# Spectral filter and gated FFN on one core: the stores of two FFT stages issued by ACT instead of SP

## The chip, the cores and the metric

The kernel runs on one core of one Trainium2 chip. The metric is the device time of the whole program in microseconds (us); lower is better. The kernel before takes 1571.36 us, the median of 3 runs (1568.31 to 1573.47).

## What is computed

Eight sequences of 3136 positions and 256 channels (`x`, float32) pass through two blocks. The first multiplies each channel's spectrum by a learned filter:

```python
X = np.fft.rfft(x, axis=1)
y = np.fft.irfft(X * (filt_r + 1j * filt_i)[None], n=3136, axis=1)
```

The second is a gated feed-forward block with a three-tap convolution along the sequence, width 1024 in the middle:

```python
h = np.maximum(y @ w_in, 0.0)
conv_out = sum(conv_w[k] * hp[:, k:k + S] for k in range(3))   # hp: h padded by one on each side
out = (h * sigmoid(conv_out)) @ w_out
```

## The kernel before

**The spectral part.** Each FFT of 3136 points is taken as 28 x 112 and done by matrix products with constant tables, in three stages that follow one another per sequence ("batch", b = 0 to 7). A batch is cut into 14 pieces of two columns (p = 0 to 13); one piece is a tile of 112 partitions x 512 float32, 224 KB. Between the stages the data must change its layout from one kind of row to another, and that is done by a trip through DRAM:

- **First stage** (`first`, matmul L321): a piece `x` is loaded from the input (L304), multiplied into a PSUM tile `ps`, copied by ACT into an SBUF tile `sa` (L309) and stored to the DRAM tensor `a_dram` of its batch (L315).
- **Second stage** (`second`, L328, for the last piece of a batch L331): a piece `a` is loaded from `a_dram` (L304) across all the rows of the batch. So the first `a` load of a batch can start only when all 14 `sa` stores of that batch have landed. Its product `pp` is multiplied by the filter on DVE (L340 to L342) and added on POOL to `z` (L344).
- **Third stage** (`third`, L351): `z` is multiplied into another `ps`, copied by ACT to `sb` (L309) and stored to `b_dram` (L315).
- **Last stage** (L216): pieces `br` are loaded back from `b_dram`, multiplied, and split by ACT (L146) and DVE (L149) into two halves `y` for the next block. For batch 0 this runs at the end of the spectral part, for the others inside the FFN part.

**The loop.** One loop of 135 steps (`i`, L369) runs all of it as a pipeline. In step i the first stage works on piece i - 1 counted over all batches, the second on piece i - 19, the third on piece i - 22. A step in the middle holds one matmul group of each stage, two ACT copies, one group of DVE and POOL work, and four transfers: load `x`, load `a`, store `sb`, store `sa`. In its first third the loop also loads the tables and the filter, and about every twelve steps a pair of weight pieces `raw` (256 KB each, L263).

**Buffers.** `x` has 8 tiles, `a` 5, `sa` and `sb` 4 each, and the PSUM tiles `ps` 5, shared by the first and third stages. An `x` load of step i waits until PE has done the first stage of the same step, because that frees its tile. An `a` load of step i is used by the second stage of step i + 4.

**What sets the order.** PE, ACT, DVE and POOL run their instructions in the order of the code (`manual_schedule` with `COMPUTE`, L368 and L527). SP runs only transfers, and their order is made by the tile framework, which simulates the program and lets SP take what it thinks is ready first. An engine's queue is strictly in order: a transfer whose wait is not met holds back everything behind it on that engine. Each transfer reports its landing on one of eight counters (DMAHW0 to DMAHW7), taken in turn over all transfers of the program in the framework's order, whichever engine issues them; a transfer waits until the one before it on its counter has landed. So about eight transfers can be under way.

**The FFN part** (from L494 on) runs from about 386 us to the end and is not touched by the edit.

Of the kernel before, what the change touches and what calls it, by code (L numbers as in the profile page):

```python
# [124 lines left out]
def tile_fft_filter_gated_ffn(  # L125
# [16 lines left out]
    nc = tc.nc  # L142
# [85 lines left out]
    with (  # L228
# [66 lines left out]
        def pool(kind):  # L295
            return xp if kind in ("x", "sa") else fp
# [10 lines left out]
        def store(kind, b, p, ps):  # L307
            st = pool(kind).tile([112, 2, D], F32, name=kind, bufs=4)
            nc.scalar.activation(st, ps, AF.Copy)  # L309
            sl = slice(2 * p, 2 * p + 2)  # L310
            if kind == "sa":
                v = a_dram[b][sl].rearrange("n p d -> p n d")
            else:
                v = b_dram[b].rearrange("n (r g) d -> (n r) g d", g=G)[:, sl]
            nc.sync.dma_start(out=v, in_=st)  # L315

        def first(b, p):
            r = rows.pop(("x", b, p))
# [49 lines left out]
        with tc.manual_schedule(engines=COMPUTE):  # L368
            for i in range(NI):  # L369
# [25 lines left out]
                if pt is not None:  # L395
                    store("sb", *at(m - 4), pt)
                if pf is not None:
                    store("sa", *at(f - 1), pf)
# [167 lines left out]
```

## Time and profile before

| | |
|---|---|
| Median of 3 runs | 1571.36 us |
| The profiled execution | 1572.45 us |
| its span in the trace | 1570.7 us |
| PE busy | 1505.0 us, 96% |
| DVE busy | 1280.6 us, 82% |
| ACT busy | 1189.3 us, 76% |
| Spectral part | 0 to about 386 us |
| of it with all three stages at work | about 80 to 326 us |

Busy times are sums over the span. A matmul's end is modelled, so PE's busy time is not PE at its peak; the distance from one matmul group's start to the next is the safer number. A row of SP's queue (SPq) shows the time in which SP issues a transfer, not the time in which the data moves.

### The profile page before, as it was taken

Reading aid. Unit: us, or ns where it says so; the run is one execution under the profiler, and the core shown is the slowest. Engines: PE = TensorE matmul, PEld = TensorE weight load, DVE = VectorE, ACT = ScalarE, POOL = GpSimd, SP = SyncE. Lnnn points to the kernel's source line nnn. Section 1 sums busy time; section 2 is a strip of 40 time slices with the busy share of each in tenths; the row PEclk is TensorE's granted clock in tenths of the full one; section 3 lists DMA queues with packets and bytes.
Section 4 is the critical chain, followed back from the end, with each engine's and each line's share of the span. In section 5 each row is a group of like instructions: output and inputs, shape, how many; then the busy total and the mean of one; then the engine's idle time right before and its main releaser. Section 6 shows DMA issues by size and latency. Waiting matters only on the chain.

```text
span 1570.7 us, 26429 instructions
## 1 busy us (share of the span) xinstructions
PE 1505.0 (96%) x9424; PEld 1346.7 (86%) x9424; DVE 1280.6 (82%) x1965; ACT 1189.3 (76%) x2162; POOL 697.4 (44%) x624
## 2 busy tenths in 40 slices
PE   5699999988999999999999999999999999999998
PEld 3356666656999999999999999999999999999998
DVE  0478888888888888888888888888888888888887
ACT  3444444435888888888888888888888888888887
POOL 0255555553444444444444444444444434444444
PEclk9799999999999999999999999999999999999999
DMA  9999999984111011111101111111111111100001
GB/s 285 288 321 337 342 342 346 328 283 140 30 48 48 30 48 48 48 48 48 47 25 36 48 53 48 47 45 47 36 42 48 48 43 36 48 25 24 24 25 48
DMA packets 128278, 166.83 MB, mean 106 GB/s; under 512 B 10682, under 2 KB 87571, under 8 KB 128147
## 3 DMA queue, kind: packets, MB, share of 16 engines
q1 hardware_dynamic: 128147, 165.14, 33.0%
q8 instruction: 75, 1.23, 0.3%
q14 instruction: 56, 0.46, 0.1%
HBM read 88.03 MB, written 77.07 MB: 105 GB/s over the span
## 4 chain that ended last, share of the span: by engine, by line
PE 83%; DMA 10%; DVE 3%; issue 1%; ACT 1%; SPq 1%; POOL 1%; ACTq 0%; DVEq 0%; POOLq 0%
PE ps_h L178 12%; PE ps_h L179 12%; PE ps_h L177 11%; PE po L473 11%; PE po L475 11%; PE po L474 11%; PE ps_h L216 6%; DMA a<-a_dram 4%; PE pp L328 3%; PE ps L351 3%; PE ps L321 2%; DMA a_dram<-sa 2%; DMA t_sb<-in_fi 1%; DVE y L149 1%; DVE v L341 1%
## 5 line engine op out<-in xcount | busy, mean ns | idle before, releaser
L152 POOL TENSOR_TENSOR g<-t,g 128x448 fp32r<-128x448 f32 x448 | 517.2, 1154 | 666.9 <-ACT g L146 262.8
L473 PE MATMUL po<-wo,g 128*128 128x256 f32 x1568 | 441.6, 282 | 0.0
L475 PE MATMUL po<-wo,g 128*128 128x256 f32 x1568 | 433.9, 277 | 0.0
L474 PE MATMUL po<-wo,g 128*128 128x256 f32 x1568 | 433.6, 277 | 0.0
L447 DVE SCALAR_TENSOR_TENSOR t<-ps_h,cw,t 128x448 f32<-128x448 f32 x448 | 305.5, 682 | 83.2 <-ACT t L442 72.9
L178 PE MATMUL ps_h<-y,wi 128*128 128x450 f32 x896 | 330.4, 369 | 4.5 <-DVE y L149 4.5
L177 PE MATMUL ps_h<-y,wi 128*128 128x450 f32 x896 | 328.8, 367 | 3.0 <-ACT y L146 1.6
L179 PE MATMUL ps_h<-y,wi 128*128 128x450 f32 x896 | 328.8, 367 | 0.0
L448 DVE SCALAR_TENSOR_TENSOR t<-ps_h,cw,t 128x448 f32<-128x448 f32 x448 | 306.4, 684 | 16.0
L442 ACT ACTIVATE t<-ps_h,cw 128x448 f32<-128x448 f32 x448 | 284.8, 636 | 42.6 <-ACT ps_h L440 1.9
L473 PEld LDWEIGHTS po<-wo,g 128*128 128x128 f32 x1568 | 294.8, 188 | 7.0
L474 PEld LDWEIGHTS po<-wo,g 128*128 128x128 f32 x1568 | 294.4, 188 | 5.7
L475 PEld LDWEIGHTS po<-wo,g 128*128 128x128 f32 x1568 | 294.5, 188 | 0.0
L440 ACT ACTIVATE ps_h<-ps_h 128x450 f32<-128x450 f32 x448 | 252.0, 562 | 31.6 <-PE ps_h L179 26.8
L453 DVE TENSOR_TENSOR t<-ps_h,t 128x448 f32<-128x448 f32 x448 | 275.1, 614 | 0.1
L452 ACT ACTIVATE t<-t 128x448 f32<-128x448 f32 x448 | 255.0, 569 | 12.2 <-DVE t L448 11.2
L146 ACT ACTIVATE g<-t 128x448 fp32r<-128x448 f32 x448 | 254.6, 568 | 0.2 <-DVE t L453 0.2
L344 POOL TENSOR_TENSOR z<-u,v 120x512 f32<-120x512 f32 x112 | 157.0, 1402 | 181.4 <-DVE v L342 164.8
L309 ACT ACTIVATE sb<-ps 112x512 f32<-112x512 f32 x112 | 66.9, 597 | 161.5 <-DMA b_dram<-sb 86.7
L179 PEld LDWEIGHTS ps_h<-y,wi 128*128 128x128 f32 x896 | 168.3, 188 | 13.9
L177 PEld LDWEIGHTS ps_h<-y,wi 128*128 128x128 f32 x896 | 170.1, 190 | 11.6 <-ACT y L146 2.8
L178 PEld LDWEIGHTS ps_h<-y,wi 128*128 128x128 f32 x896 | 168.3, 188 | 13.5 <-DVE y L149 6.7
(51 smaller groups left out, 1475.0 us busy)
## 6 DMA issues: line engine op xcount, KB each, us to landing
x<-in_x SPq DMA_DIRECT2D x112, 224.0 KB, 4.9
a_dram<-sa SPq DMA_DIRECT2D x112, 224.0 KB, 4.6
a<-a_dram SPq DMA_DIRECT2D x112, 224.0 KB, 4.6
b_dram<-sb SPq DMA_DIRECT2D x112, 224.0 KB, 4.4
br<-b_dram SPq DMA_DIRECT2D x112, 224.0 KB, 2.6
out<-ot SPq DMA_DIRECT2D x27, 896.0 KB, 4.1
raw<-in_w_in SPq DMA_DIRECT2D x8, 256.0 KB, 5.2
raw<-in_w_out SPq DMA_DIRECT2D x8, 256.0 KB, 6.1
```

The lines of the kernel that those rows point to most:

```text
L152: nc.gpsimd.tensor_tensor(out=dst, in0=src, in1=hi.bitcast(F32), op=ALU.subtract)
L177: nc.tensor.matmul(ps, lhsT=wh, rhs=rh, start=start, stop=False, **kw)
L178: nc.tensor.matmul(ps, lhsT=wh, rhs=rl, start=False, stop=False, **kw)
L179: nc.tensor.matmul(ps, lhsT=wl, rhs=rh, start=False, stop=stop, **kw)
L442: nc.scalar.activation(t, h[:, 1:SUB + 1], AF.Copy, scale=cw[:, 1, f:f + 1])
L447: nc.vector.scalar_tensor_tensor(out=t, in0=h[:, 0:SUB], scalar=cw[:, 0, f:f + 1], in1=t, op0=ALU.mult, op1=ALU.add)
L448: nc.vector.scalar_tensor_tensor(out=t, in0=h[:, 2:SUB + 2], scalar=cw[:, 2, f:f + 1], in1=t, op0=ALU.mult, op1=ALU.add)
L452: nc.scalar.activation(t, t, AF.Sigmoid)
L453: nc.vector.tensor_mul(t, h[:, 1:SUB + 1], t)
L473: nc.tensor.matmul(o, lhsT=gh[:, sl], rhs=wo[0][:, f], start=first, stop=False, skip_group_check=True)
L474: nc.tensor.matmul(o, lhsT=gh[:, sl], rhs=wo[1][:, f], start=False, stop=False, skip_group_check=True)
L475: nc.tensor.matmul(o, lhsT=gl[:, sl], rhs=wo[0][:, f], start=False, stop=last, skip_group_check=True)
```

## The change

The store at the end of `store` (L315) is issued from ACT's queue instead of SP's. `store` is called for `sb` and `sa` in each step, so 224 stores move. Each one now stands on ACT directly behind the copy that fills its tile.

```diff
             if kind == "sa":
                 v = a_dram[b][sl].rearrange("n p d -> p n d")
             else:
                 v = b_dram[b].rearrange("n (r g) d -> (n r) g d", g=G)[:, sl]
-            nc.sync.dma_start(out=v, in_=st)
+            nc.scalar.dma_start(out=v, in_=st)
```

In the rows of order below, the names are those of the trace with a buffer's number: a_dram_62 is batch 5, a_dram_63 batch 6, a_dram_64 batch 7. The words in brackets are the counters that an instruction waits for: DMAHW for transfers, PE and Activation for those engines.

ACT, around the last `sa` piece of batch 5 (the 84th of 112), in the kernel before:

```order
L309 ACTIVATE sa<-ps 112x512 [waits DMAHW1_49,PE_49,Activation_49]
L309 ACTIVATE sb<-ps 112x512 [waits DMAHW4_49,PE_49,Activation_49]
L309 ACTIVATE sa<-ps 112x512 [waits DMAHW5_49,PE_49,Activation_49]
L309 ACTIVATE sb<-ps 112x512 [waits DMAHW0_49,PE_49,Activation_49]
L309 ACTIVATE sa<-ps 112x512 [waits DMAHW1_49,PE_49,Activation_49]
```

The same place on ACT in the changed kernel:

```order
L309 ACTIVATE sa<-ps 112x512 [waits PE_49]
L315 DMA a_dram_62<-sa 112x2x256 [waits DMAHW6_49,Activation_49]
L309 ACTIVATE sb<-ps 112x512 [waits PE_49]
L315 DMA b_dram_69<-sb 112x512 [waits DMAHW7_49,Activation_49]
L309 ACTIVATE sa<-ps 112x512 [waits PE_49]
L315 DMA a_dram_62<-sa 112x2x256 [waits DMAHW1_49,Activation_49]
L309 ACTIVATE sb<-ps 112x512 [waits DMAHW5_49,PE_49]
L315 DMA b_dram_69<-sb 112x512 [waits DMAHW2_49,Activation_49]
```

Each copy is followed by its store, which waits for that copy and for an earlier transfer on its counter; most copies no longer wait for a transfer themselves.

SP, at the same place, where the second stage goes from batch 4 (a_dram_61) to batch 5 (a_dram_62), in the kernel before:

```order
L304 DMA x<-in_x 112x512 [waits DMAHW6_49,PE_49]
L304 DMA a<-a_dram_61 112x512 [waits DMAHW7_49]
L315 DMA b_dram_69<-sb 112x512 [waits DMAHW0_49,Activation_49]
L315 DMA a_dram_62<-sa 112x2x256 [waits DMAHW1_49,Activation_49]
L263 DMA raw<-in_w_in 128x512 [waits DMAHW2_49,DVE_49]
L263 DMA raw<-in_w_out 128x512 [waits DMAHW3_49]
L304 DMA x<-in_x 112x512 [waits DMAHW4_49,PE_49]
L304 DMA a<-a_dram_62 112x512 [waits DMAHW5_49,DMAHW1_49]
L315 DMA b_dram_69<-sb 112x512 [waits DMAHW6_49,Activation_49]
L315 DMA a_dram_63<-sa 112x2x256 [waits DMAHW7_49,Activation_49]
L304 DMA x<-in_x 112x512 [waits DMAHW0_49,PE_49]
L304 DMA a<-a_dram_62 112x512
```

The changed kernel, from the `x` load beside the last a_dram_61 load on:

```order
L304 DMA x<-in_x 112x512 [waits DMAHW6_49,PE_49]
L304 DMA a<-a_dram_61 112x512 [waits DMAHW3_49,DMAHW0_49,PE_49]
L304 DMA x<-in_x 112x512 [waits DMAHW2_49,PE_49]
L304 DMA x<-in_x 112x512 [waits DMAHW5_49,PE_49]
L304 DMA x<-in_x 112x512 [waits DMAHW0_49,PE_49]
L304 DMA x<-in_x 112x512 [waits DMAHW7_49,DMAHW3_49,PE_49]
L304 DMA a<-a_dram_62 112x512 [waits DMAHW6_49,DMAHW7_49,DMAHW5_49,DMAHW1_49]
L304 DMA a<-a_dram_62 112x512
L304 DMA a<-a_dram_62 112x512 [waits DMAHW0_49]
L304 DMA x<-in_x 112x512 [waits DMAHW2_49,PE_49]
L304 DMA a<-a_dram_62 112x512 [waits DMAHW4_49,DMAHW3_49]
L304 DMA a<-a_dram_62 112x512 [waits DMAHW5_49,PE_49]
```

Without the stores SP's queue holds loads alone. In the kernel before, the first a_dram_62 load follows directly on the `x` load of its own step; in the changed kernel it stands behind three further `x` loads, and then three `a` loads come together. Its wait for several DMAHW counters is the wait for the `sa` stores of its batch, which ACT now issues.

## Rows read from the trace of the kernel before

**Rows 1.** The page: traffic in 40 equal slices of the span:
```profile
GB/s 285 288 321 337 342 342 346 328 283 140 30 48 48 30 48 48 48 48 48 47 25 36 48 53 48 47 45 47 36 42 48 48 43 36 48 25 24 24 25 48
```

**Rows 2.** Stretches: busy us of PE, PEld, DVE, ACT, POOL; clock, DMA share, GB/s:
```profile
100.00:320.00 220.00, 206.08 (x790) 137.88 (x789) 184.48 (x279) 96.29 (x168) 125.59 (x97) 1.00 1.00 339
...
226.00:252.00 26.00, 26.00 (x102) 17.86 (x101) 23.13 (x35) 12.82 (x23) 15.37 (x13) 1.00 1.05 370
...
252.00:262.00 10.00, 9.03 (x38) 6.17 (x37) 8.42 (x14) 3.40 (x6) 5.53 (x4) 1.00 0.93 292
...
346.00:386.00 40.00, 34.20 (x174) 25.79 (x173) 34.34 (x46) 19.73 (x28) 14.16 (x11) 0.98 0.63 189
...
386.00:1570.00 1184.00, 1175.37 (x8168) 1127.77 (x8167) 1004.55 (x1552) 1022.93 (x1891) 518.13 (x476) 1.00 0.13 41
```

**Rows 3.** Chain that ended last, in order of time: start us, us, what:
```profile
242.98 0.86 PE pp L328 x2
243.84 0.86 PE ps L351 x4
244.70 0.86 PE ps L321 x4
```

**Rows 4.** PE's waits, 100 to 320: us in total, times, longest us:
```profile
PE pp L328 <- DMA a<-a_dram: 12.1, 14, 1.9
```

**Rows 5.** ACT's waits, 100 to 320:
```profile
ACT sb L309 <- DMA b_dram<-sb: 83.2, 53, 4.1
```

**Rows 6.** SP's waits, 100 to 320:
```profile
SPq L304 <- DMA a_dram<-sa: 13.2, 6, 3.8
```

**Rows 7.** ACT's groups, 100 to 320: busy us, mean ns, idle before:
```profile
L309 ACT ACTIVATE sb<-ps 112x512 f32<-112x512 f32 x78 | 46.6, 597 | 114.3 <-DMA b_dram<-sb 83.2 <-PE ps L351 16.6 <-PE ps L321 12.9
L309 ACT ACTIVATE sa<-ps 112x512 f32<-112x512 f32 x78 | 46.6, 597 | 9.9 <-DMA a_dram<-sa 4.1 <-PE ps L321 4.0 <-PE pp L328 0.7
```

**Rows 8.** Issues of L315 and L304, 100 to 320: ns min/median/max; landing:
```profile
L315 SPq DMA_DIRECT2D b_dram<-sb x80: 303/416/1458, 99.7 to 319.3; - x80
...
L315 SPq DMA_DIRECT2D a_dram<-sa x79: 317/380/1287, 100.1 to 317.9; - x79
...
L304 SPq DMA_DIRECT2D a<-a_dram x79: 303/741/1612, 101.1 to 318.4; - x79
...
L304 SPq DMA_DIRECT2D x<-in_x x73: 317/454/1287, 100.6 to 305.1; - x73
...
DMA to landing us min/median/max: 2.9/4.7/6.2
```

**Rows 9.** SP's queue in order of time: start us, us, instruction:
```profile
248.06 0.37 SPq L315 DMA_DIRECT2D a_dram<-sa  x1
...
250.06 0.38 SPq L304 DMA_DIRECT2D x<-in_x  x1
...
253.02 0.32 SPq L304 DMA_DIRECT2D a<-a_dram  x1
```

**Rows 10.** ACT in order of time: the 84th copy to sa:
```profile
243.07 0.60 ACT L309 ACTIVATE sa<-ps 112x512 f32<-112x512 f32 x1 [0.27 <-PE ps L321]
```

**Rows 11.** ACT in the FFN part: an instruction that waits for ACT's own result:
```profile
422.15 0.53 ACT L440 ACTIVATE ps_h<-ps_h 128x450 f32<-128x450 f32 x1
422.77 0.64 ACT L442 ACTIVATE t<-ps_h,cw 128x448 f32<-128x448 f32 x1
```

**Rows 12.** All engines in order of time: first copy to sa, its store:
```profile
8.61 0.60 ACT L309 ACTIVATE sa<-ps 112x512 f32<-112x512 f32 x1 [1.77 <-PE ps L321]
...
9.59 0.33 SPq L315 DMA_DIRECT2D a_dram<-sa  x1
```

**Rows 13.** Chain in order of time, at the spectral part's end:
```profile
347.69 1.00 DVE y L149
...
350.75 1.02 DVE y L149
```

**Rows 14.** A group of ACT, 346 to 386:
```profile
L146 ACT ACTIVATE y<-ps 128x448 fp32r<-128x448 f32 x13 | 13.1, 1007 | 0.0
```

## The prediction, made before the changed kernel was run

> **What bounds the kernel now.** I looked first at where the edited line runs. The table of stretches shows two programs in one span: from 386 us on PE is busy for 1175 of 1184 us with 41 GB/s of traffic, and before that the traffic is 285 to 346 GB/s for some 320 us [rows 1, 2]. The stores of L315 are in the second one alone, so the FFN part can change by nothing but its starting time, and everything below is about the first 386 us.
>
> In the stretch from 100 to 320 us all three stages work. ACT made 78 copies to `sb` there [rows 7], so a step takes 220 / 78 = 2.82 us. Two limits lie close below it. The chain shows PE's three groups one directly after the other, 0.86 us each [rows 3]: 2.58 us per step if nothing waits. And the transfers: 339 GB/s on the mean, but 370 in the good stretch from 226 to 252 us, where the DMA share is 1.05 and PE never idle [rows 2]. At 370 the same bytes would take 220 x 339 / 370 = 201.6 us; PE alone would take 78 x 2.58 = 201.2 us. Both say the same: at most some 18.5 us can be won here, and below that two limits wait together.
>
> Where do the 18.5 us go? PE's own waits name `a` loads, 12.1 us in 14 waits [rows 4]. SP's waits say why: its longest are for `sa` stores to land before an `a` load, 13.2 us in 6 waits, one for each change of batch [rows 6]. The change to batch 5 shows the pattern. The 84th copy to `sa`, the last of batch 5, starts at 243.07 and takes 0.60 [rows 10]; its store (the 84th) is issued only at 248.06, since SP is two steps behind; the first `a` load of that batch goes out at 253.02, 3 us after the load ahead of it [rows 9]. In the ten microseconds after it traffic falls to 292 GB/s [rows 2], which costs 10 x (1 - 292/370) = 2.1 us. Six of these make 12.6 us, close to PE's 12.1. The other 5.9 us I put down to the weight pieces and small gaps.
>
> ACT is not a limit: 1.19 us of copies per step [rows 7]. It waits a lot, 83.2 us for `sb` stores [rows 5], but only because those stores are late; nobody waits for it in turn for long.
>
> **The change, part by part.** *Stores leave SP.* SP issues 2 transfers per step instead of 4, and stores go out with their copy. The store of the 84th copy would be issued near 243.8 instead of 248.06 and land, 4.7 us later as loads and stores do at the median [rows 8], near 248.5. This takes away the six waits of SP for `sa` stores.
>
> What is late next? By the order shown for SP, the first `a` load of a batch now stands behind three more `x` loads. The last of these waits for PE's first stage of its step, and the second stage that needs the `a` load comes one step later: PE has the second, third and first groups in between, 3 x 0.86 = 2.6 us. The `x` issue takes 0.45 us, and the `a` load lands 2.9 us (shortest) to 4.7 us (median) after its issue [rows 8]. So PE waits 0.45 + 0.05 + 2.9 - 2.6 = 0.8 us to 2.6 us at each change of batch. I take 1.2, near the short end, since for three steps before it only three transfers per step went out (3 x 229 KB / 2.58 us = 267 GB/s, under the 370 that is possible), so that no queue stands in front of it. Six times 2.1 - 1.2 gives 5.4 us won; with the ends, 6 x 1.3 = 7.8 us won to 6 x -0.5 = 3.0 us lost.
>
> *Weight pieces.* SP's queue has the `raw` pair in front of the next `x`, `a` and, before, of the two stores. Stores now pass it, loads don't. Of the 5.9 us I count half, 3 us won; ends 0 and 5.9.
>
> *Stores arrive on ACT.* 224 issues, two per step, each behind its own copy, with that copy's result as a wait. No row shows ACT issuing a transfer. From SP's medians an issue is 0.42 us for `sb` and 0.38 for `sa` [rows 8]. The nearest row for the wait is ACT waiting for ACT: 422.77 - (422.15 + 0.53) = 0.09 us [rows 11]; the far one is SP waiting for ACT's copy at the very start, 9.59 - (8.61 + 0.60) = 0.38 us [rows 12]. With the near one a step on ACT is 2 x 0.60 + 0.42 + 0.38 + 4 x 0.09 = 2.36 us, under the 2.58 of PE: hidden, cost 0. With the far one before both issues it is 2.94 us, over today's 2.82: 78 x 0.12 = 9.4 us lost, and no gain. I take 0, as the wait is one of ACT for itself. Queued behind a store on ACT are the next copies and, about every twelve steps, the weight splits of L146; the five `ps` tiles let PE run about two steps ahead of a late copy.
>
> The Trainium skill speaks against this cover: by Perfetto Trace Analysis, section on the HWDGE DMA instruction, the descriptor generator is locked for exclusive use by one sequencer at a time, and the wait for the lock is part of the issue's row. The long `a` issues on SP (median 0.741 us [rows 8]) would fit a full queue as well; no row here has two issuers. By the page, an ACT issue could have to sit out an SP issue; this is a reason for the far end, not a term of the sum.
>
> *Before 100 us.* The stretch is filled with transfers at 285 to 321 GB/s [rows 1]. Stores that no longer queue behind table loads might mix better: if 80 us ran at 339 instead of 286, 80 x (1 - 286/339) = 12.5 us would be won. Nothing shows that the order is the cause of the low rate, so 0; I keep 6 us of it for the range.
>
> *From 326 to 386 us.* DVE sets a step of 350.75 - 347.69 = 3.06 us [rows 13]. ACT has one copy, one store and one `y` of 1.01 us [rows 14]: 0.60 + 0.42 + 1.01 + 3 x 0.09 = 2.3 us. Hidden, 0.
>
> **The sum.** 5.4 + 3 = 8.4 us won, of which ACT's hiccups may take a little: -8 us on the profiled execution, 1572.45 - 8 = 1564.5 us. The median lies 1.1 us lower, at 1571.36, so I predict 1563 us.
>
> **Rivals.** *The same bound in another place (no change).* The 16 DMA engines are at a share of 1.00 from 100 to 320 us, and the rate in a good stretch is only 9% above the mean [rows 2]. If the first `a` load of a batch waits 2.1 us behind its three `x` loads (within the 0.8 to 2.6 above) and the idle slots there are not made up later, the six changes of batch cost what they cost now: 1571 us. For it: the order itself. Against it: PE's 14 waits for `a` go with SP being behind, and SP now has half its work. The Trainium skill says so too, in DMA: Bandwidth & Descriptors, section "Issuing engines are not separate DMA queues": transfers from any engine run on the same 16 engines and interleave, and a second issuer only saves issue time. The trace agrees that the engines are full (share 1.00), and by that rule the time would stay near 1571.
>
> *ACT becomes the bound (slower).* Place: ACT's queue, copy, wait, issue, copy, wait, issue. Price: at the far wait 2.94 us per step; with the issues as long as SP's `x` issues (0.45) it is 2 x 0.60 + 2 x 0.45 + 2 x 0.38 + 2 x 0.09 = 3.04 us, 78 x 0.22 = 17 us lost, 1571 + 17 = 1588 us; in between, 1580. It decides from a step of 2.82 us on ACT on, that is, from 0.23 us more per store than I count. For it: the far row, and issues of over 1 us on SP in full queues (maxima 1.3 to 1.6 [rows 8]); a blocked issue now blocks copies. Against it: if ACT were the limit, the queues would be emptier and the issues short again.
>
> *A better mix (faster by more).* With the `x` loads early and stores out of the way all of the 18.5 us come back, and some of the 6 us before 100: 1571 - 21 = 1550 us.
>
> **Chances and range.** Forecast, 1555 to 1566 us: 0.40. Better mix: 0.08. Same bound: 0.24. ACT bound: 0.28. A measurement of this kernel can tell about 0.3% (4.7 us) from no change. Faster by more than that: 0.46, the two first cases but for a corner of 0.02; within it: 0.25; slower: 0.29, ACT's case and a part of the waits for `a` at their far end. The range of 8 in 10 is 1552 to 1585; the likeliest case alone, 1555 to 1566.
>
> **What the changed profile would show.** Right: no waits of SP for a_dram<-sa of several microseconds; the store of the 84th copy issued within 0.5 us of its end; more than 80 copies to `sb` between 100 and 320 us; PE's waits for `a` under 9 us, each near 1 us; ACT's waits for b_dram<-sb (83.2 us) nearly gone; GB/s there near 353. The issue on ACT should be near 0.4 us and the gap before it near 0.1. Wrong: PE waiting for ACT's `ps` (L351 or L321 behind `sa` or `sb`), ACT's issues and gaps adding to over 1.6 us a step, or the same 2 us lost at each change of batch with SP waiting for PE in place of a store. A granted clock below 1.00 between 100 and 320 us would be something I have not reckoned with.

## The result, and the profile after

The changed kernel takes 1576.05 us (median of 6 runs, 1574.79 to 1577.95); the kernel before took 1571.27 us beside it (6 runs, 1568.31 to 1573.47). The ratio is 1.003, 95% interval 1.002 to 1.004: slower by 0.3%, where 1563 us and a gain were predicted. The profiled execution after took 1575.70 us with a span of 1573.9 us, 3.2 us more than the span before.

First the same stretches as in [rows 2]; the columns are those of there:

```profile
100.00:320.00 220.00, 206.51 (x774) 136.15 (x773) 180.77 (x272) 96.24 (x167) 124.39 (x96) 0.98 1.01 336
...
386.00:1570.00 1184.00, 1178.61 (x8175) 1130.66 (x8175) 1004.20 (x1553) 1023.76 (x1892) 518.60 (x476) 1.00 0.13 40
```

The FFN part runs as before, only later. Between 100 and 320 us the traffic is 336 GB/s instead of 339, and the granted clock fell from 1.00 to 0.98. Then PE's waits, 100 to 320 us, which answer to [rows 4]:

```profile
PE ps L321 <- ACT sb L309: 8.4, 9, 2.4
PE ps L351 <- ACT sa L309: 3.9, 6, 2.1
PE pp L328 <- DMA a<-a_dram: 0.6, 2, 0.4
```

The waits for `a` went from 12.1 us to 0.6, and waits for ACT, of which PE had none before, took their place: 12.3 us in 15 waits, the longest 2.4 us instead of 1.9. ACT's waits in the same stretch answer to [rows 5]:

```profile
ACT sb L309 <- DMA a<-a_dram: 22.3, 11, 5.7
...
ACT sa L309 <- DMA x<-in_x: 12.3, 10, 3.4
...
ACT sb L309 <- DMA b_dram<-sb: 0.6, 1, 0.6
```

The 83.2 us that ACT waited for `sb` stores are gone. But now its copies wait for *loads* to land, though a copy out of PSUM reads no load. What waits is the store in front of the copy. The issues on ACT and SP themselves became short, as one sees beside [rows 8]:

```profile
L315 ACTq DMA_DIRECT2D b_dram<-sb x78: 321/321/386, 99.8 to 318.9; - x78
L315 ACTq DMA_DIRECT2D a_dram<-sa x78: 311/312/906, 101.7 to 319.9; - x78
```

```profile
L304 SPq DMA_DIRECT2D a<-a_dram x77: 303/311/1352, 101.0 to 318.4; - x77
L304 SPq DMA_DIRECT2D x<-in_x x71: 312/317/1765, 102.3 to 304.0; - x71
```

One place shows the whole chain. ACT in order of time:

```profile
198.08 0.60 ACT L309 ACTIVATE sa<-ps 112x512 f32<-112x512 f32 x1 [0.46 <-PE ps L351]
201.96 0.31 ACTq L315 DMA_DIRECT2D a_dram<-sa  x1
202.32 0.60 ACT L309 ACTIVATE sb<-ps 112x512 f32<-112x512 f32 x1 [3.64 <-DMA a<-a_dram]
```

and PE in order of time:

```profile
202.97 1.20 PE L321 MATMUL ps<-x,s_sb 112*112 112x256 f32 x4 [2.40 <-ACT sb L309]
203.96 1.91 PE L328 MATMUL pp<-a,s_sb 112*120 112x512 f32 x2
205.66 1.83 PE L351 MATMUL ps<-z,i_sb 120*112 120x256 f32 x4
207.33 1.03 PE L321 MATMUL ps<-x,s_sb 112*112 112x256 f32 x4
```

The `sa` copy ends at 198.68. Its store goes out only at 201.96, 3.28 us later. It waits until the transfer before it on its landing counter has landed; here that is an `a` load which SP issued at 195.65 and which landed at 201.88. The next copy stands behind the store, PE finds no free `ps` and waits 2.40 us. After that its groups start 1.70 us apart instead of 0.86: the granted clock is 0.50 from 204 to 206 us, the lower of the two levels (1.2 GHz), for 3.4 us, which costs another 1.7 us. The clock in tens of microseconds shows this twice between 100 and 320 us, and in the kernel before not at all:

```profile
120.00:130.00 10.00, 9.06 (x29) 5.98 (x30) 5.73 (x9) 4.46 (x8) 4.02 (x4) 0.83 1.07 338
200.00:210.00 10.00, 7.61 (x24) 4.70 (x23) 4.62 (x7) 4.38 (x9) 4.87 (x5) 0.83 0.99 325
```

The one at 120 us has the same history: an `sb` store blocked 3.00 us by an `x` load, then PE idle for 2.14 us.

```profile
119.78 0.32 ACTq L315 DMA_DIRECT2D b_dram<-sb  x1
120.20 0.60 ACT L309 ACTIVATE sa<-ps 112x512 f32<-112x512 f32 x1 [3.42 <-DMA x<-in_x]
...
120.94 1.09 PE L351 MATMUL ps<-z,i_sb 120*112 120x256 f32 x4 [2.14 <-ACT sa L309]
```

So all of PE's waits between 100 and 320 us are 13.7 us before and 13.2 us after, but (1 - clock) x 10 us, summed, adds 0 before and 3.4 us after. What the stretch lost as a whole is read from PE's third stage, from its 13th to its 93rd group, in the kernel before and then in the changed one:

```profile
99.23 1.03 PE L351 MATMUL ps<-z,i_sb 120*112 120x256 f32 x4
...
324.36 1.12 PE L351 MATMUL ps<-z,i_sb 120*112 120x256 f32 x4 [0.22 <-POOL z L344]
```

```profile
98.73 1.03 PE L351 MATMUL ps<-z,i_sb 120*112 120x256 f32 x4
...
328.07 1.12 PE L351 MATMUL ps<-z,i_sb 120*112 120x256 f32 x4 [0.21 <-POOL z L344]
```

These 80 pieces took 225.1 us before and 229.3 us after. Of the 4.2 us, some 1.6 are won back by the last group, near 380 us, and the span grew by 3.2 us; that 3.4 and 3.2 lie so close is partly chance. The clock by stretches is known for this one execution only. Over the six executions of the changed kernel the mean granted clock of the whole span was 0.984 to 0.990, and the time does not follow it (1575.51 us at 0.990, 1575.70 us at 0.984). So that the clock decides the median is not shown.

### The profile page after: what moved, and what is told of

Its sections match the earlier page's. It is cut to its first block, busy times and chain, and to the rows that moved or that the text cites. A ratio compares the mean times of both kernels' runs of the same rounds, so it can differ in the third digit from the quotient of the medians.

```text
span 1573.9 us, 26330 instructions
## 1 busy us (share of the span) xinstructions
PE 1510.8 (96%) x9424; PEld 1351.0 (86%) x9424; DVE 1280.7 (81%) x1965; ACT 1192.6 (76%) x2162; POOL 698.0 (44%) x624
## 4 chain that ended last, share of the span: by engine, by line
PE 83%; DMA 9%; DVE 4%; ACT 2%; issue 1%; ACTq 0%; POOL 0%; SPq 0%; DVEq 0%; POOLq 0%
PE ps_h L178 12%; PE ps_h L179 12%; PE ps_h L177 11%; PE po L473 11%; PE po L475 11%; PE po L474 11%; PE ps_h L216 5%; PE ps L321 4%; DMA x<-in_x 3%; PE ps L351 3%; PE pp L328 3%; DMA a<-a_dram 2%; DMA a_dram<-sa 2%; DVE y L149 1%; DVE v L341 1%
## 5 line engine op out<-in xcount | busy, mean ns | idle before, releaser
L452 ACT ACTIVATE t<-t 128x448 f32<-128x448 f32 x448 | 255.1, 569 | 12.2 <-DVE t L448 11.0
L179 PEld LDWEIGHTS ps_h<-y,wi 128*128 128x128 f32 x896 | 168.6, 188 | 13.9
L149 DVE TENSOR_TENSOR y<-ps_h,y 128x448 fp32r<-128x448 f32 x98 | 103.1, 1052 | 76.7 <-ACT y L146 76.7
```

What stands on the lines that cost most here:

```text
L179: nc.tensor.matmul(ps, lhsT=wl, rhs=rh, start=False, stop=stop, **kw)
L452: nc.scalar.activation(t, t, AF.Sigmoid)
```

## The experiments

Three theories. *Counter*: a store on ACT waits for the landing of whatever had its counter before, blocks the copies behind it, and PE runs out of `ps`. *Order*: SP's `a` loads are late since they stand behind `x` loads that wait for PE. *Full engine*: the 16 DMA engines set the pace whoever issues.

The two kernels and the twelve experiments in one table: time (median), ratio to the kernel before with its interval, and from 100 to 320 us PE's waits for `a`, for `ps` behind ACT, in all, and what the fallen clock cost. The last four columns are read from the one profiled execution, whose time lies up to 5.4 us off the median (1576.83 us with the stores on GpSimd). The clock column is the sum of (1 - clock) x 10 us; it counts PE's idle time at the lower level too and is an upper bound. The before medians beside them were 1573.09, 1572.99 and 1572.70 us in the three groups.

| kernel | us | ratio | a | ps | all | clock |
|---|---|---|---|---|---|---|
| before | 1571.27 | 1 | 12.1 | 0 | 13.7 | 0 |
| after | 1576.05 | 1.0030 [1.0020, 1.0040] | 0.6 | 12.3 | 13.2 | 3.4 |
| sa on ACT | 1567.36 | 0.9959 [0.9945, 0.9973] | 5.9 | 3.2 | 9.4 | 0 |
| sb on ACT | 1574.58 | 1.0017 [1.0005, 1.0029] | 9.3 | 0.4 | 9.7 | 3.4 |
| SP in written order | 1576.58 | 1.0026 [1.0013, 1.0040] | 0.5 | 11.9 | 13.3 | 5.1 |
| stores on GpSimd | 1571.44 | 0.9996 [0.9984, 1.0009] | 4.4 | 0 | 9.8 | 3.4 |
| after, 4 ps | 1577.53 | 1.0025 [1.0016, 1.0034] | 0.2 | 12.3 | 12.5 | 3.4 |
| before, 4 ps | 1572.64 | 1.0003 [0.9994, 1.0012] | 14.5 | 0 | 16.6 | 0 |
| copies first | 1568.37 | 0.9967 [0.9956, 0.9979] | 1.1 | 6.6 | 8.1 | 0 |
| sa ACT, sb GpSimd | 1566.81 | 0.9960 [0.9944, 0.9976] | 3.0 | 0 | 5.1 | 0 |
| after, x later | 1577.72 | 1.0035 [1.0020, 1.0049] | 1.4 | 13.9 | 15.3 | 3.4 |
| before, x later | 1571.57 | 0.9996 [0.9983, 1.0009] | 12.2 | 0 | 12.2 | 1.7 |
| loads on GpSimd | 1605.47 | 1.0216 [1.0189, 1.0242] | 0 | 0 | 24.9 | 16.4 |
| sb on ACT, behind | 1573.21 | 0.9991 [0.9975, 1.0007] | 10.9 | 0 | 10.9 | 5.1 |

### The two halves of the change, the order on SP, another issuer

Only the `sa` stores on ACT:
```
+            (nc.scalar if kind == "sa" else nc.sync).dma_start(out=v, in_=st)
```


> Only the sa stores are issued by ACT, the sb stores stay on SP. Counter theory (a store on ACT waits for its landing counter, whose transfer before is often one of SP's loads; the copies behind it wait too, and PE then lacks a PSUM tile): half as many such waits on ACT, PE's waits for ACT between 100 and 320 us fall from 12.3 us to about 6, time between the two kernels, 1572 to 1575 us. Order theory (a loads stand behind x loads on SP, which wait for PE): time as in the changed kernel if SP's order at a change of batch keeps the three x loads in front, 1575 to 1577 us. Full-engine theory (the 16 DMA engines set the pace): 1571 to 1574 us, no matter which half.

Only the `sb` stores on ACT:
```
+            (nc.scalar if kind == "sb" else nc.sync).dma_start(out=v, in_=st)
```


> Only the sb stores are issued by ACT, the sa stores stay on SP. Counter theory: as for the sa half, 1572 to 1575 us, with ACT's waits behind sb stores alone. Order theory: SP still waits for ACT's copies before its sa stores, so that its queue is late again and the a loads wait for late sa stores: 1572 to 1577 us. Full-engine theory: 1571 to 1574 us.

The changed kernel with SP's instructions too in the order in which they are written:
```
-        with tc.manual_schedule(engines=COMPUTE):
+        with tc.manual_schedule(engines=COMPUTE | {mybir.EngineType.SP}):
```


> The changed kernel, with SP's queue in the order of the code in the spectral part (x, a, x, a, also at a change of batch). Order theory: the a loads no longer stand behind three x loads, SP's waits for PE's first stage (55.6 us) fall and the time comes to 1560 to 1571 us. Counter theory: ACT's stores still share their counters with loads (65 of 224 stores have an x or a load before them on their counter, 89 in the changed kernel), so a little better at most: 1572 to 1576 us, and PE's waits for ACT remain at 6 to 12 us.

All stores on GpSimd's queue, which has counters of its own:
```
+            nc.gpsimd.dma_start(out=v, in_=st)
```


> All sa and sb stores are issued by POOL. POOL's transfers have counters of their own, so that no store waits for a load, and ACT issues nothing. Counter theory: PE's waits for ACT vanish, and if POOL's issues are no dearer than its idle time (it is busy 125 of 220 us) the time falls under the kernel before, 1558 to 1569 us. Order theory: SP's queue holds loads alone as in the changed kernel, so PE's loss stays: 1573 to 1578 us. Full-engine theory: 1569 to 1574 us. If POOL's issues cost over 0.6 us each, z comes late and it is slower, over 1580 us, and says nothing on the counters.

The halves part: `sa` alone wins 0.4%, `sb` alone loses 0.2%. PE's waits with `sa` alone and then with `sb` alone, 100 to 320 us:

```profile
PE pp L328 <- DMA a<-a_dram: 5.9, 8, 1.6
PE ps L321 <- ACT sb L309: 3.2, 5, 1.3
```

```profile
PE pp L328 <- DMA a<-a_dram: 9.3, 8, 2.7
PE ps L351 <- ACT sa L309: 0.4, 2, 0.2
```

So the gain that was predicted exists, and belongs to the `sa` stores: they are what an `a` load waits for. None of the three theories had expected it; all had `sa` alone at 1571 us or more. The `sb` stores have no reader before the last stage. What `sb` alone loses is, in its profiled execution, lost early: from 80 to 100 us the traffic is 277 GB/s and the clock 0.83, against 303 and 0.91 before, and the 13th group of the third stage starts 5.1 us behind the kernel before, the 93rd only 2.9 us. The order theory falls: SP's order changed and its waits for PE's first stage fell from 55.6 to 33.2 us, the time did not change, and PE waits for ACT as long as in the changed kernel. The full-engine theory had 1571 to 1574 us whichever half moved; both halves lie outside, `sa` alone well below. With the stores on GpSimd PE never waits for ACT, but the gain that the counter theory expected did not come: GpSimd is busy for 211.99 of 220 us and PE waits 5.4 us for its `z`:

```profile
PE ps L351 <- POOL z L344: 5.4, 13, 0.8
...
L315 POOL DMA_DIRECT2D b_dram<-sb x78: 572/572/637, 99.8 to 318.0; - x78
L315 POOL DMA_DIRECT2D a_dram<-sa x78: 677/677/780, 100.4 to 318.5; - x78
```

### Where the store stands, and how much cover there is

The changed kernel and the kernel before with one `ps` tile less:
```
-        tc.tile_pool(name="fps", bufs=5, space=bass.MemoryType.PSUM) as fps,
+        tc.tile_pool(name="fps", bufs=4, space=bass.MemoryType.PSUM) as fps,
```


> The changed kernel with 4 ps tiles in PSUM instead of 5 (nothing else). Blocked-copies theory: stores on ACT sit in front of the copies until the transfer before them on their landing counter is in (53 of the 206 steady ones for over 0.3 us, the longest 5.3 us), PE goes on only as long as free ps tiles last; each tile is half a step, 1.3 us of cover, so with one less the waits of PE for ps behind ACT (12.3 us from 100 to 320 us in the changed kernel) at least double, to 25 to 45 us, and the time is 1588 to 1608 us. Full-engine theory (the 16 DMA engines set the pace, ACT's blocking is only where their backlog shows): PE has to wait anyway, so the tile count matters little: 1574 to 1580 us.

> The control: the kernel before (all stores on SP) with 4 ps tiles instead of 5. Blocked-copies theory: here it is SP that sits out the landings, ACT copies follow PE closely, so one tile less costs little: 1570 to 1578 us, PE's waits for ps behind ACT under 5 us, and in any case the loss is less than half of what the changed kernel loses by the same edit. Full-engine theory: the same loss in both, within 3 us of each other.

The changed kernel with both copies of a step ahead of both stores:
```
 in store:   - nc.scalar.dma_start(out=v, in_=st)
             + late.append((v, st))
 in the loop, behind the two calls of store:
             + while late:
             +     v, st = late.pop(0)
             +     nc.scalar.dma_start(out=v, in_=st)
```


> The changed kernel with both copies of a step first on ACT and then both stores (copy sb, copy sa, store sb, store sa instead of copy, store, copy, store). Blocked-copies theory: a blocked sb store no longer stands in front of the sa copy of its own step, so of two places where a blocked store holds a copy only one is left; PE's waits for ps behind ACT fall from 12.3 to some 6 us between 100 and 320 us and the time to 1569 to 1573 us. If the blocking sums up whatever the place: 1575 to 1578 us as in the changed kernel. ACT-issue theory (the issues themselves take ACT's time): no change either, 1575 to 1578.

`sa` stores on ACT, `sb` stores on GpSimd:
```
+            (nc.scalar if kind == "sa" else nc.gpsimd).dma_start(out=v, in_=st)
```


> sa stores on ACT, sb stores on GpSimd's queue with landing counters of its own (104 of the 112 sb stores then follow an sb store on their counter), loads on SP. Blocked-copies theory: ACT has one store per step as in the run with sa stores alone (1567.4 us), SP waits for no store, and ACT's waits for sb buffers (56 us there between 100 and 320 us) go: 1560 to 1567 us, as far as GpSimd's additional issue (0.57 us per sb store in the run with all stores there) does not hold up the z additions. Full-engine theory: no better than sa alone, 1566 to 1571 us.

What came to be tested here is what a blocked store does to the copies behind it (blocked copies), and by how much the `ps` tiles cover that. The cover is not what counts: with four tiles both kernels take the time they took with five. The blocked-copies expectation missed by over 10 us, the full-engine theory had these times right, and why one tile less is free was not settled. The place counts for more. With the copies first 1576 us become 1568.37 us. Its ACT in order of time:

```profile
200.06 0.60 ACT L309 ACTIVATE sb<-ps 112x512 f32<-112x512 f32 x1 [3.70 <-PE ps L353]
200.56 0.59 ACT L309 ACTIVATE sa<-ps 112x512 f32<-112x512 f32 x1
200.86 0.32 ACTq L403 DMA_DIRECT2D b_dram<-sb  x1
202.78 0.36 ACTq L403 DMA_DIRECT2D a_dram<-sa  x1
203.19 0.60 ACT L309 ACTIVATE sb<-ps 112x512 f32<-112x512 f32 x1 [2.04 <-DMA a<-a_dram]
```

and PE's and ACT's waits, 100 to 320 us (L323 and L353 are L321 and L351 of the other kernels):

```profile
PE ps L323 <- ACT sb L309: 6.6, 10, 1.5
```

```profile
ACT sb L309 <- PE ps L353: 27.5, 16, 4.0
```

The stores are blocked no less. Between 100 and 320 us the sum over all stores on ACT, from the end of ACT's instruction before to the issue, is 86.5 us here (a store issued before that end counted as 0) and 62.5 us in the changed kernel. But the `sa` copy no longer stands behind a blocked `sb` store, PE's longest wait is 1.5 us, the clock stays at 1.00, and ACT's copies to `sb` wait 27.5 us for PE's third stage (4.0 us in the changed kernel; all of ACT's waits for PE are 60.8 us here and 49.5 there). So a blocked issue has no price by its length; it costs what it keeps from the engine that needs it.

The place is not all that this edit changed. SP's order came out different too: at a change of batch two `x` loads stand in a row where the changed kernel has three or four, and SP's waits for PE's first stage are 7.8 us instead of 55.6:

```profile
SPq L304 <- PE ps L323: 7.8, 21, 1.2
```

That SP's order alone does not bring the gain is shown by the run with SP in written order (1576.58 us). The place with SP's order held was not run.

With `sb` on GpSimd PE waits least of all, 5.1 us, and its first FFN matmul starts at 372.31 us instead of 382.60. The span is only 6.3 us shorter than before, since in that execution 7.2 us lie between the last issue of an output store and the end, against 3.1 us before; the rows do not say what fills them. Its time, 1566.81 us, lies in the expected ranges of both theories and does not part them.

### The links of the chain, one by one

The changed kernel and the kernel before with the `x` loads one step later:
```
-                if (bp := at(f + 7)) and i:
+                if (bp := at(f + 6)) and i > 1:
```


> The changed kernel with each x load written one step later (six steps ahead of its use instead of seven; with eight x tiles its tile then is free a step before it is asked for). Ring theory: in the changed kernel the three queues wait for each other in a ring: SP's x load for PE to free the x tile (SP waits 55.6 us for L321 from 100 to 320 us, against 4.6 before the change), PE for ACT to copy ps out (12.3 us), ACT's store for the landing of one of SP's loads on the same counter (40.6 us); taking the first link away lets SP run ahead: SP's waits for PE's L321 fall under 15 us, PE's waits for ACT under 6 us, time 1566 to 1572 us. Place theory (only where the store stands in ACT's row matters): nothing changes there, 1574 to 1578 us. Full-engine theory: 1574 to 1578 us.

> The control: the kernel before (stores on SP) with the same edit, x loads one step later. Ring theory: there is no ring here (SP waits 4.6 us for PE's L321), so nothing to win: 1569 to 1574 us. If the later x loads are simply a better mix for the DMA engines, this kernel gains as much as the changed one does, some 5 us or more: 1563 to 1567 us.

The changed kernel with the loads on GpSimd:
```
-            nc.sync.dma_start(out=r, in_=v[:, 2 * p:2 * p + 2])
+            nc.gpsimd.dma_start(out=r, in_=v[:, 2 * p:2 * p + 2])
```


> The changed kernel with the x and a loads issued by GpSimd, on landing counters of its own; SP keeps weights and tables, ACT's stores follow stores on their counters from the second batch on (of 224 some 34 follow something of SP). Counter theory (the link from SP's loads to ACT's stores is the shared counter): what ACT's stores wait for loads goes from 40.6 us to near 0, ACT's stores are blocked for under 35 us in all from 100 to 320 us instead of 62.5, PE's waits for ps behind ACT are under 4 us instead of 12.3. In exchange GpSimd's z additions stand behind x loads that wait for PE, so PE waits for z by 5 to 15 us; time 1566 to 1578 us. If ACT's stores are blocked for the DMA engines' backlog and not for the counter, ACT's blocking stays at 55 us or more and PE's waits for ps near 12.

`sb` stores alone on ACT, behind both copies (the edit is shown against the kernel with both copies first):
```
             - late.append((v, st))
             + late.append((v, st)) if kind == "sb" else nc.sync.dma_start(out=v, in_=st)
```


> sb stores alone on ACT, as in the run that took 1574.58 us, but with the store behind both copies of the step (copy sb, copy sa, store sb) instead of between them; sa stores on SP. Place theory: a store between the copies is what costs; behind both it costs nothing, and the gain of a shorter SP queue is left as with sa alone: 1566 to 1571 us. Otherwise 1573 to 1576 us as before.

Two readings were left: a ring of three queues that wait for each other, and the place of the store in ACT's row. The ring is not settled: with `x` later SP waits for PE as long as without the edit, so the edit did not take away the link that it was meant to, and the time says nothing on the ring. SP's waits in the changed kernel and with `x` later:

```profile
SPq L304 <- PE ps L321: 55.6, 46, 2.2
```

```profile
SPq L304 <- PE ps L321: 59.4, 51, 2.5
```

The counter link is borne out. Among the changed kernel's stores from 100 to 320 us, 59 have a load before them on their counter and are blocked for 40.6 us, 90 have a store and are blocked for 19.2. With the loads on GpSimd no store follows an `x` or `a` load any more, 126 follow a store and are blocked for 3.8 us, 14 follow one of SP's other loads and are blocked for 16.6. PE never waits for ACT:

```profile
PE ps L351 <- POOL z L344: 24.9, 10, 5.7
```

The time of that kernel, 27 us above its expected range, says nothing on the counter: `z` now stands behind loads on GpSimd, and the clock adds up to 16.4 us. Its landings are not shorter, though its DMA engines are less full (share 0.93): ACT's stores land after 5.2 us at the median, 4.3 us in the changed kernel. But its steps are longer (220 / 70 = 3.1 us), and two transfers a step go over the counters of SP and ACT instead of four, so that the same counter comes round later. So the counter is shown as the place where ACT waits; that it is a load there, and not the number of transfers on the counters, that makes the wait long is not separated. `sb` behind both copies ends ACT's part (no wait of PE for ACT), yet the time is 1573.21 us, above what was expected. Five of the twelve executions took 1565.79 to 1569.56 us, nearly all as expected; the other seven, the profiled one (1574.03 us) among them, 1573.04 to 1575.47 us. In the profiled one the `sa` stores, still on SP, are late, and PE still waits 10.9 us for `a`, with waits up to 2.4 us and three falls of the clock (5.1 us):

```profile
PE pp L330 <- DMA a<-a_dram: 10.9, 8, 2.4
```

What sets the five apart was not profiled.

## Why the prediction was wrong

*What bounds the kernel: right.* Only the first 386 us changed.

*Stores leave SP: the mechanism right, the size too small.* 5.4 us were counted for the six changes of batch; the waits for `a` fell by 11.5 us. The store of the 84th copy goes out 0.03 us behind it, as predicted, but the copy itself starts 9.3 us later than before:

```profile
252.41 0.60 ACT L309 ACTIVATE sa<-ps 112x512 f32<-112x512 f32 x1 [0.40 <-PE pp L328]
253.04 0.31 ACTq L315 DMA_DIRECT2D a_dram<-sa  x1
```

The wait of 0.8 to 2.6 us behind three `x` loads did not come: at this change of batch PE waits 0.25 us.

```profile
261.84 1.09 PE L328 MATMUL pp<-a,s_sb 112*120 112x512 f32 x2 [0.25 <-DMA a<-a_dram]
```

Three groups were counted between PE's first stage that frees the last `x` tile and the second stage that needs the `a` load; the trace has six there. SP still waits for a_dram<-sa, in 12 waits instead of 6 [rows 6]; the test "no such waits" failed, though PE no longer pays for them.

```profile
SPq L304 <- DMA a_dram<-sa: 12.8, 12, 3.4
```

*Weight pieces* were not measured apart.

*Stores arrive on ACT: this step failed.* It priced an issue (0.42 us) and the wait of a store for its own copy (0.09), and got 0 because 2.36 us fit into PE's 2.58. Both rows were better than priced: 0.31 us and 0.03 us. Missing was a third thing that a store waits for, the landing of the transfer before it on its counter. The rows of order on ACT already had it, as a DMAHW counter beside the Activation counter of each store; the sum priced the second alone and left the first at nothing without a reason. It came to 62.5 us over 155 stores, 0.40 us each on the mean and up to 5.27. In the kernel before SP sat out these waits, and no copy stood behind SP. The sentence "five `ps` tiles let PE run about two steps ahead of a late copy" did not hold either: a block of 3.28 us reached PE as a wait of 2.40 us.

*The clock* was named as something not reckoned with. In the profiled execution PE waits about as much as before, two of its waits are over 2 us long, and up to 3.4 us of clock come on top; that this decides the median is not shown.

*The rivals.* ACT as the bound had the sign right and the time (1580 to 1588 us) too high. Its price was laid on throughput and far waits for the copy; the runs show ACT with time to spare (copies and issues make 2 x 0.60 + 2 x 0.31 = 1.8 us of a 2.8 us step) and a blocked place in its row. The Trainium skill's rule in Perfetto Trace Analysis, section on the HWDGE DMA instruction, that the descriptor generator is locked for exclusive use and the wait for it is part of the issue's row, does not show in the medians: with two issuers they fell to 0.31 to 0.32 us on both queues. Single rows of up to 1.77 us on SP remain. *Same bound elsewhere* is not what happened: with the same bytes to move the issuer and the place moved the time from 1576 to 1567 us. By the Trainium skill, DMA: Bandwidth & Descriptors, section "Issuing engines are not separate DMA queues", a second issuer saves only issue time; that does not part the kernels of 1576, 1568 and 1567 us, all of which issue stores from ACT.

*The other tests:* 77 copies to `sb` instead of over 80, and 336 GB/s instead of 353, both missed; waits for b_dram<-sb nearly gone (0.6 us) and PE waiting for ACT's `ps`, the sign named for "wrong", were both seen.

## What to carry to other kernels

When a transfer's issue moves to a compute engine, price three things: the issue, the wait for its data, and the wait for the transfer before it on its completion counter; then look at what stands behind it in that engine's row. Put stores behind all copies that another engine is waiting for (here 1576 us became 1568 us by that edit, which also changed SP's order), and move only those whose readers wait (here `sa` alone, 1567 us). Look at the granted clock beside PE's waits: in the profiled executions here about the same sum of waits came once without a fall of the clock and once with two.

## What was unexpected of the hardware

A wait of TensorE of 2.14 or 2.40 us was followed by 3.4 us at 1.2 GHz, a loss of 1.7 us each time, while fourteen waits for `a` of up to 1.9 us in the kernel before cost no clock between 100 and 320 us. The length of the wait alone does not tell: in the run with `x` later the clock fell behind a wait of 1.73 us at 188.61 us too. An issue row on ACT lasted 0.31 us even with the DMA engines at a share of 1.01, where SP's had medians of 0.38 to 0.74 us when it issued all four transfers of a step.
